# An attention-and-two-layers kernel: another order of the first layer, 65 operations on other engines, 14 dummy products, another order of PSUM tiles, and a wider constant

## The chip, the cores and the metric

The kernel runs on one core of a Trainium2 chip. The metric is the device time of one launch in microseconds (us), the median of the runs; smaller is better. Engines in the profile: PE is TensorE's matmuls and PEld its weight loads, DVE is VectorE, ACT is ScalarE, POOL is GpSimd, SP is SyncE, which here only issues DMA transfers. PEclk is the clock that the throttle granted to TensorE, as a share of full speed.

## The reference

Attention over 32 memory slots, then two layers of a gated kind. Batch 4, 8 heads, 576 positions, head width 64; 2304 tokens, model width 512, inner width 1536.

```python
a = np.exp(phi - np.max(phi, axis=2, keepdims=True))          # over the 576 positions
a = a / (np.sum(a, axis=2, keepdims=True) + 1e-09)
k_m = np.einsum('bhsm,bhsd->bhmd', a, k)
v_m = np.einsum('bhsm,bhsd->bhmd', a, v)
scores = scale * np.matmul(q, k_m.transpose(0, 1, 3, 2))
attn = np.exp(scores - np.max(scores, axis=-1, keepdims=True))
attn = attn / (np.sum(attn, axis=-1, keepdims=True) + 1e-09)
x = np.matmul(attn, v_m)                                       # then to 2304 x 512
x = (x @ w_a) * (x @ w_b) @ w_out                              # first layer
g = x @ w_gate                                                 # second layer
return g * (1.0 / (1.0 + np.exp(-g))) * (x @ w_val) @ w_out
```

The layers' weights arrive as 64-bit floats, seen as pairs of 32-bit words; the kernel turns them into 32-bit floats itself.

## The kernel before, in words

Every operand of a large product is held as two fp32r tiles, a high part and a low one (`hi`, `lo`), and each product is three: high by high, high by low, low by high. One launch has two halves: attention and the first layer, up to about 398 us, and the second layer.

**Weights.** A chunk of weights i.j is loaded by `W` (i is a block of 128 of the inner width, j which of three matrices) and decoded by `chunk`, in steps: absolute value and low word on ACT (L222, L224), a clamp (L228) on DVE or POOL, two DVE operations (L232, L236), an add on POOL (L246 or L248), and for output weights a high part on ACT and a low part (`o_lo`) on POOL.

**Attention**, for each batch b: `att_phi` takes the maximum of phi over the nine groups r of positions (`over_r`, L320 to L326: four operations, of which the first two have 384 elements), transposes it on PE (L336), takes it further on DVE and PE, adds, takes the exponential (L355), and makes k_m and v_m on PE in one bank (L364, called kv in the profile); `att_sum` adds phi's exponentials; then the scaled parts are transposed (L399) and copied out (L406, two copies, on ACT). `att_q` transposes q (L424; 8, 8 and 2 blocks) and copies it; `att_scores` makes the scores of two head pairs on PE (L442 and L452), and takes maximum, exponential, sum and quotient on DVE and ACT. Each batch has two such blocks. `att_out` transposes the weights of attention back (L489).

**First layer.** v_m is multiplied into w_a and w_b first (`vw_part`, L543). `s1_a` and `s1_b` are the products with 288 columns (L528); s1b's result is copied by ACT (L594), multiplied on DVE (L596), and split (L603, and L608 on DVE or POOL). `s2_first` and `s2_part` multiply by w_out (L520, 384 columns) and add into an accumulator, on DVE (L645). `x_ops` makes the operands of the second layer from the accumulators (L671 to L679, high and low parts on DVE and POOL).

**Second layer.** `second` closes the first layer's pools and opens a PSUM pool `ps2` of eight banks. `unit` works through seven products p5, p1, p2, p6, p3, p7, p4 with 288 columns (L776; p_z, p_a and p_c in the profile are their banks), and `s4_tile` is the last product (L520, 512 columns, p_h).

**Order.** The work is written as generators, and `PLAN` is a hand-written list of tokens. Each occurrence of a token runs its generator to the next `yield`: P, K, L, Q and W are loads (phi, k and v of two head pairs, of the other two, q, weights), p the steps of `att_phi`, e `att_sum`, q `att_q`, s `att_scores`, o `att_out`, c a chunk's, v `vw_part`, a and b `s1_a` and `s1_b`, d and f `s2_first` and `s2_part`, x `x_ops`, E `second`, U a `unit`, A and O later loads and H `s4_tile`. At the end `behind` chains the instructions of each engine, SP too, in the plan's order, so each engine's queue is the plan. `STEPS` holds for some operations a letter for the engine of each occurrence (A, V, P). The function `warm` exists, but the plan of before does not use it. A tile of a `ring` takes a buffer of its tag in rotation where `SLOTS` has no entry for it, and `SLOTS` is empty; the tag b2 has four PSUM buffers of two banks each.

`const` holds the identity `ident` (128x128, the moving operand of all transposes) and behind it `ones`, two columns of fp32; all other tiles are placed behind these.

Of the kernel before, what the change touches and what calls it, by code (L numbers as in the profile page):

```python
# [1113 lines left out]
```

## Time and profile before

| what | us |
|---|---|
| median of three runs | 822.45 |
| runs | 824.23, 822.04, 822.45 |
| the profiled execution | 822.6 |
| its span in the trace | 820.8 |
| PE busy | 795.0 (97%) |
| DVE busy | 573.4 (70%) |
| ACT busy | 403.6 (49%) |
| POOL busy | 381.7 (47%) |

The span is the time from the first instruction to the last in the trace of the profiled execution; the rest of its 822.6 lies outside the trace. A busy share is that of instructions that compute or move data on the engine; waits are not in it.

### The profile page before, as it was taken

How to read it: one execution, taken by the hardware profiler on the slowest of the kernel's cores; microseconds unless marked ns; L12 is line 12 of the kernel's file. 1: busy time of each engine (PE TensorE's matmuls, PEld its weight loads, DVE VectorE, ACT ScalarE, POOL GpSimd, SP SyncE). 2: the span in 40 equal slices, each digit the busy share in tenths (PEclk: the TensorE clock that was granted, in tenths of full speed). 3: DMA queues.
4: the chain of work that ended last, by engine and by line, in shares of the span. 5: the costliest groups of instructions: out<-in, count | busy, mean ns of one | idle time of the engine just before them, and what ended most of it. 6: DMA issues, size and time to landing. Idle time of an engine off the chain costs nothing.

```text
span 820.8 us, 16480 instructions
## 1 busy us (share of the span) xinstructions
PE 795.0 (97%) x6540; PEld 745.9 (91%) x6540; DVE 573.4 (70%) x1020; ACT 403.6 (49%) x790; POOL 381.7 (47%) x319
## 2 busy tenths in 40 slices
PE   3799999999999999999899999999999999999997
PEld 2688999999999999999899999999999999999996
DVE  5899967878866777488685767856786455656565
ACT  3556656346434543354467565444464653434331
POOL 1454665545535354355667646544563442424210
PEclk9899999999999999999999999999999999999999
DMA  9984233543433323211456546323233422113004
GB/s 326 378 300 141 91 123 130 174 143 112 143 100 102 105 77 122 72 39 46 128 168 230 163 153 200 108 91 110 91 86 103 129 70 72 47 56 129 20 1 115
DMA packets 61772, 102.51 MB, mean 125 GB/s; under 512 B 6400, under 2 KB 35072, under 8 KB 61696
## 3 DMA queue, kind: packets, MB, share of 16 engines
q1 hardware_dynamic: 60896, 100.29, 37.6%
q8 instruction: 51, 0.84, 0.4%
q10 hardware_dynamic: 800, 1.18, 0.4%
q14 instruction: 25, 0.20, 0.1%
HBM read 82.58 MB, written 18.87 MB: 124 GB/s over the span
## 4 chain that ended last, share of the span: by engine, by line
PE 94%; DMA 2%; DVE 2%; SPq 1%; issue 0%; ACT 0%
PE p_a L776 19%; PE p_h L520 18%; PE s L520 15%; PE p_z L776 9%; PE s1a L528 9%; PE s1b L528 9%; PE p_c L776 5%; PE s L528 3%; PE vw L543 2%; DMA h10x<-in_phi_dram 1%; PE sc L442 1%; DMA h7x<-in_q_dram 1%; PE qT L424 1%; SPq L312 1%; PE kv L364 1%; PE sc L452 0%
## 5 line engine op out<-in xcount | busy, mean ns | idle before, releaser
L520 PE MATMUL p_h<-o,g 128*128 128x512 f32 x648 | 163.2, 393 | 0.0
L520 PEld LDWEIGHTS p_h<-o,g 128*128 128x128 f32 x648 | 117.0, 188 | 21.0 <-DVE h_2x L851 0.2
L520 PE MATMUL s<-gh,o 128*128 128x384 f32 x480 | 125.3, 335 | 0.0
L248 POOL TENSOR_TENSOR dec_a<-dec_a,raw 128x512 int32<-128x512 int32 x48 | 65.3, 1364 | 83.2 <-DVE dec_a L236 47.6
L520 PEld LDWEIGHTS s<-gh,o 128*128 128x128 f32 x480 | 87.0, 188 | 0.8 <-issue 0.4
L851 DVE TENSOR_TENSOR h_2x<-p_h,h_2x 128x512 f32<-128x512 f32 (+1 forms) x100 | 62.1, 633 | 35.8 <-PE p_h L520 35.4
L222 ACT ACTIVATE dec_a<-raw 128x512 f32<-128x512 f32 x72 | 48.4, 677 | 69.4 <-DMA dr_o<-dec_a 16.5
L520 PE MATMUL s<-gl,o 128*128 128x384 f32 x240 | 80.2, 334 | 0.0
L528 PE MATMUL s1b<-h_1x,vwh 128*128 128x288 f32 x384 | 67.6, 298 | 0.0
L528 PE MATMUL s1a<-h_1x,vwh 128*128 128x288 f32 x384 | 67.2, 297 | 0.1
L528 PEld LDWEIGHTS s1b<-h_1x,vwh 128*128 128x128 f32 x384 | 56.5, 188 | 3.5 <-issue 3.3
L246 POOL TENSOR_TENSOR w<-dec_a,raw 128x512 int32<-128x512 int32 x24 | 31.9, 1331 | 59.0 <-DVE dec_a L236 31.9
L528 PEld LDWEIGHTS s1a<-h_1x,vwh 128*128 128x128 f32 x384 | 56.5, 189 | 1.4 <-issue 0.8
L236 DVE SCALAR_TENSOR_TENSOR dec_a<-raw,dec_a 128x512 int32<-128x512 int32 x72 | 53.7, 746 | 2.5
L596 DVE TENSOR_TENSOR bs<-s1a,bs 128x576 f32<-128x576 f32 x48 | 36.0, 753 | 24.6 <-PE s1a L528 22.3
L594 ACT COPY bs<-s1b 128x576 f32<-128x576 f32 x48 | 30.4, 639 | 43.8 <-PE s1b L528 36.5
L161 POOL TENSOR_TENSOR w_g<-again_a,w_g 128x512 fp32r<-128x512 f32 x24 | 31.7, 1322 | 43.4 <-ACT w_g L157 40.8
L161 POOL TENSOR_TENSOR w_u<-again_s,w_u 128x512 fp32r<-128x512 f32 x24 | 31.9, 1328 | 40.8 <-ACT w_u L157 40.8
L827 ACT CAST g<-gate 128x576 fp32r<-128x576 f32 x48 | 32.1, 676 | 36.2 <-PE p_h L520 21.1
L794 DVE TENSOR_TENSOR p_c<-p_c,gate 128x288 f32<-128x288 f32 x48 | 22.1, 465 | 38.6 <-PE p_c L776 27.9
L829 DVE TENSOR_TENSOR g<-gate,g 128x576 fp32r<-128x576 f32 x48 | 38.7, 811 | 14.7 <-ACT g L827 14.2
L603 ACT CAST gh<-bs 128x576 fp32r<-128x576 f32 x48 | 31.0, 673 | 34.0 <-PE s L520 29.9
(224 smaller groups left out, 1943.4 us busy)
## 6 DMA issues: line engine op xcount, KB each, us to landing
raw<-in_moe_w_out_dram SPq DMA_DIRECT2D x24, 512.0 KB, 3.5
again_s<-dr_w SPq DMA_DIRECT2D x24, 512.0 KB, 3.7
dr_w<-dec_a SPq DMA_DIRECT2D x36, 256.0 KB, 3.3
again_a<-dr_w SPq DMA_DIRECT2D x24, 384.0 KB, 3.1
raw<-in_moe_w_b_dram SPq DMA_DIRECT2D x12, 512.0 KB, 4.4
raw<-in_moe_w_a_dram SPq DMA_DIRECT2D x12, 512.0 KB, 3.9
raw<-in_moe_w_val_dram SPq DMA_DIRECT2D x12, 512.0 KB, 3.7
...
```

The source lines that it names most:

```text
L161: nc.gpsimd.tensor_tensor(out=t[:, :, 1], in0=x, in1=f32(t[:, :, 0]), op=ALU.subtract)
L222: nc.scalar.activation(out=f32(a), in_=f32(hi), func=ACTF.Abs)
L236: nc.vector.scalar_tensor_tensor(out=a, in0=hi, scalar=-0x40000000, in1=a, op0=ALU.bitwise_and, op1=ALU.bitwise_or)
L246: nc.gpsimd.tensor_tensor(out=o, in0=ai, in1=li, op=ALU.add)
L248: nc.gpsimd.tensor_tensor(out=a, in0=a, in1=lo, op=ALU.add)
L520: nc.tensor.matmul(dst, lhsT=l, rhs=r, start=(i == 0), stop=(i == n - 1))
L528: nc.tensor.matmul(p[:, hb, 0:HB], l, x, start=(i == 0), stop=(i == n - 1))
L596: nc.vector.tensor_tensor(out=bs, in0=pa_t.pop((b, f)), in1=bs, op=ALU.mult)
L776: nc.tensor.matmul(bank(where), lhsT=x, rhs=y, start=first and t == 0, stop=t == len(terms) - 1, skip_group_check=True,)
L827: nc.scalar.copy(out=hi, in_=v)
L829: tt(out=lo, in0=v, in1=f32(hi), op=ALU.subtract)
L851: tt(out=dst, in0=src, in1=dst, op=add)
```

## The change

1. `SLOTS` is filled: each tile of b2 and of the rings of raw, dec_a, pm, nmx, rs, kvm, w, mx, vwh, den, vwl, bs, o, gh, gl, q, g, s, t, g2 and a22 gets a buffer number of its own, in place of rotation.
2. `ones` is cut from a tile of 32 columns, 128 bytes to a partition in place of 8, so all tiles start at multiples of 128.
3. `o_lo` of the first layer and the copies of k (L406) take their engine from `STEPS`.
4. `STEPS`: 65 operations change engine: 25 from DVE to POOL (9 low parts at L608, 12 clamps, 2 quotient multiplies, 2 sums), 26 from POOL to DVE (7 at L608, 7 `o_lo`, 6 clamps, 4 multiplies, 2 sums), 9 from DVE to ACT (5 q copies, 4 copies of `s2_first`), 5 from ACT to DVE (2 copies of k, 1 q copy, 2 of `s2_first`).
5. `BANKS` gives the order in which the second layer's PSUM tiles are placed.
6. `PLAN` has the same tokens in another order and 14 new ones, z0 to z13, which run `warm`: a product of the identity with itself twice, 256 columns in fp32, into a b2 tile that nobody reads. The order differs up to E, in some 90 tokens behind it and in the middle of the second layer; the last 330 tokens are the same. In the new plan the loads begin P0, P1, L0, W0.1, K0, Q0, W0.0, W1.1, W1.2, K1, L1, Q1, W1.0; before they began P0, L0, W0.1, W0.0, K0, W1.1, Q0, P1, W1.2, K1, L1, W1.0, Q1. The scores s1.1 and s1.0 now come ahead of the first of a and b; before, b0.0 and b0.1 came first.

The tokens that end the first layer's DVE work are, before, f1.3, f1.2, x1, x1, f1.4, E, and now f1.3, f1.4, x1, f1.2, f1.1, E. The first `unit` after E was U0.12 and is U1.12.

```diff
     SLOTS = """
+    b2
...
+    raw
+    0123012301320132010321032130213132313203012023012013203132012302312301301320312031203121203201312032101020210321320230210
+    a 012012102021010102120120101201021022100210100212021021022102021021201102 pm 0101 nmx 0101 rs
+    0101 kvm 0101 w 012301030202130231201302312013023120130231201302312013023120 mx 01010101 vwh
...
-    ones = const.tile([128, 2], FP32, name="ones")
+    ones = const.tile([128, 32], FP32, name="ones")[:, 0:2]
...
-        nc.gpsimd.tensor_tensor(out=l, in0=x, in1=f32(h), op=ALU.subtract)
+        (eng("ol", i) if i < NF else nc.gpsimd).tensor_tensor(out=l, in0=x, in1=f32(h), op=ALU.subtract)
...
-            nc.scalar.copy(out=kb[b % 2][rows, :, :, o], in_=kT[rows])
+            copy(eng("kT", b), kb[b % 2][rows, :, :, o], kT[rows])
...
-    gl VPPVVPPPVVVPPVVVVVPPVVPVPVVVPVPPVVPVPPVVVPVPPPVV rmx VVVV mul PVPVPPPV sub VVVVVVVV sum
-    VPPV qT AAAVAVVAAAVV acc VVVAVAVAAVVVVVVA clamp VVVVVPVPPVVVPPPVVPVVPPVVVVVVVVVVPVVPVVPVVV
+    gl VPVPPVVVVVVVPVPVPVPPPVPPPVVPPVPPVPPVPPVVPVVVPPVV rmx VVVV mul VPVPPVVV sub VVVVVVVV sum
+    PVVP ol PPVVVVVVVPPP kT VAAV qT AAAAVAAAAAAA acc AAAAVAVVAVVVVVAV clamp
+    PVPVPPPPPVVPVPVVVVPVPVPPPVPVPPVVVVVVVVPVVV
...
+    BANKS = "z1 z0 a1 a0 c1 c0 h0 h1"
...
-        for n in ("a0", "c0", "z0", "a1", "c1", "z1", "h0", "h1"):
-            chain.append(ps2.tile([128, 512], FP32, tag=n, name=f"p_{n}"))
+        names = ("a0", "c0", "z0", "a1", "c1", "z1", "h0", "h1")
+        t = {n: ps2.tile([128, 512], FP32, tag=n, name=f"p_{n}") for n in BANKS.split()}
+        chain.extend(t[n] for n in names)
...
-    P0 L0 W0.1 W0.0 c0.1 c0.0 c0.0 p0 p0 K0 p0 c0.1 c0.1 p0 p0 p0 W1.1 c0.0 c0.1 Q0 p0 e0 P1 W1.2
-    p0 c1.1 c0.0 q0.0 p0 c1.1 p0 q0.0 q0.2 K1 p0 p0 q0.1 L1 p1 c1.1 p1 q0.2 p1 p0 p1 c1.1 p0 s0.0
-    W1.0 c0.1 c0.0 q0.1 p1 c1.2 p1 s0.1 s0.0 s0.0 v0 s0.0 s0.1 s0.1 v0 s0.0 s0.0 Q1 p1 v0 c1.1 e1
-    p1 W0.2 s0.0 s0.1 s0.1 P2 c1.0 c1.0 s0.1 s0.1 c1.0 c1.2 o0.1 L2 p1 q1.2 c1.0 p1 o0.1 p1 o0.0
-    o0.0 c0.2 q1.0 o0.1 c1.0 v1 W2.2 p1 q1.2 o0.0 c0.2 v1 p2 p1 b0.0 c1.2 p2 P3 v1 c0.2 b0.1 W4.1
...
+    P0 P1 L0 p1 z6 z7 p0 z9 W0.1 c0.1 p1 z0 K0 p0 p0 Q0 p0 c0.1 p0 z2 z12 z1 p1 p0 W0.0 z10 p1 W1.1
+    p1 W1.2 e0 p0 p0 c0.1 q0.2 c0.1 K1 q0.2 L1 p0 q0.1 p0 p0 c0.0 Q1 p0 z13 q0.1 c0.1 q0.0 c1.1
+    c0.0 q0.0 c1.1 p0 W1.0 s0.1 P2 s0.0 c1.2 z4 p0 W0.2 c0.0 c1.1 z8 c1.1 c0.0 z3 s0.1 z11 c0.0
+    c1.2 K2 p1 s0.1 s0.0 s0.0 s0.1 v0 z5 e1 s0.0 c1.1 v0 c1.2 s0.0 c1.2 p1 s0.1 s0.1 c1.2 p1 p1 v0
+    q1.0 q1.1 p1 q1.0 s0.0 q1.2 c1.0 W2.2 p1 s0.0 p1 s0.1 c1.0 o0.1 o0.0 W4.1 q1.2 o0.1 q1.1 p2 p1
+    c1.0 P3 c0.2 o0.0 c0.2 o0.1 c1.0 c0.2 o0.0 s1.1 s1.1 p2 p2 c1.0 p1 s1.1 s1.0 p2 L2 c1.2 v1 a0.0
...
```

## Rows read from the trace of the kernel before

**Rows 1.** The page, first part: busy us, share of the span, instructions.
```profile
PE 795.0 (97%) x6540; PEld 745.9 (91%) x6540; DVE 573.4 (70%) x1020; ACT 403.6 (49%) x790; POOL 381.7 (47%) x319
```

**Rows 2.** Windows: us; busy of PE, PEld, DVE, ACT, POOL; PEclk; DMA share; GB/s.
```profile
0.00:10.00 10.00, 1.14 (x5) 0.48 (x5) 3.08 (x10) 1.75 (x2) 0.70 (x6) 1.00 0.83 281
10.00:20.00 10.00, 5.84 (x158) 5.37 (x158) 6.86 (x14) 4.99 (x10) 2.57 (x2) 1.00 1.09 369
20.00:30.00 10.00, 7.12 (x96) 5.89 (x95) 6.57 (x13) 5.40 (x9) 2.98 (x3) 0.77 1.05 384
30.00:40.00 10.00, 7.76 (x206) 6.24 (x205) 9.46 (x22) 6.27 (x12) 5.10 (x6) 0.89 1.06 374
40.00:50.00 10.00, 10.00 (x113) 9.07 (x113) 9.19 (x18) 6.51 (x12) 4.57 (x5) 1.00 0.93 317
...
400.00:450.00 50.00, 50.00 (x350) 48.41 (x350) 33.84 (x70) 37.15 (x84) 36.75 (x33) 1.00 0.52 166
```

**Rows 3.** Waits of PE: what it waited for; us in total, times, longest.
```profile
PE mx L336 <- DVE pm L326: 9.1, 2, 6.8
...
PE p_z L776 <- DVE h8x L645: 2.6, 1, 2.6
```

**Rows 4.** The chain that ended last: start us, us, what ran.
```profile
25.97 1.05 PE sc L442 x16
...
39.90 1.59 PE s1b L528 x12
...
47.14 0.87 PE qT L424 x8
48.02 0.61 PE sc L442 x16
48.63 0.23 PE sc L452 x4
...
395.46 2.01 DVE h_x0x L679 x3
397.46 0.88 DVE h8x L645
```

**Rows 5.** Timeline of SP's queue: start us, us, issue of the second q.
```profile
18.87 7.13 SPq L312 DMA_DIRECT2D h5x<-in_q_dram  x2
```

**Rows 6.** DMA view: the same q's larger part, its size, us to landing.
```profile
h5x<-in_q_dram SPq DMA_DIRECT2D x1, 1024.0 KB, 14.7
```

**Rows 7.** Timeline of ACT in the front.
```profile
37.73 0.73 ACT L222 ACTIVATE dec_a<-raw 128x512 f32<-128x512 f32 x1
...
40.02 0.74 ACT L406 COPY kb<-kvT 64x256 f32<-64x256 f32 x2
```

**Rows 8.** Lines, the clamp on either engine: busy us, mean ns; idle before.
```profile
L228 DVE TENSOR_SCALAR dec_a<-dec_a 128x512 f32<-128x512 f32 x61 | 33.9, 563 | 4.5 <-ACT dec_a L222 4.5
L228 POOL TENSOR_SCALAR dec_a<-dec_a 128x512 f32<-128x512 f32 x11 | 21.6, 1965 | 11.4 <-ACT dec_a L222 11.4
```

**Rows 9.** Timeline of DVE ahead of the second layer.
```profile
397.38 0.95 DVE L645 TENSOR_TENSOR h8x<-s,h8x 128x768 f32<-128x768 f32 x1
```

**Rows 10.** Timeline of POOL and DVE at 13 us; in brackets idle before, releaser.
```profile
13.45 1.28 POOL L246 TENSOR_TENSOR w<-dec_a,raw 128x512 int32<-128x512 int32 x1 [12.15 <-DVE dec_a L236]
13.90 1.25 DVE L323 TENSOR_TENSOR rm<-h9x 128x384 f32<-128x384 f32 x1 [0.59 <-ACT h9x L355]
15.18 0.56 DVE L324 TENSOR_TENSOR rm<-rm,h9x 128x384 f32<-128x384 f32 x1
```

**Rows 11.** The chain again: long products of the second layer.
```profile
674.40 3.22 PE p_a L776 x24
...
805.67 10.90 PE p_h L520 x48
```

**Rows 12.** Timeline of PE: two blocks of vw products, eight at a time.
```profile
51.35 1.09 PE L543 MATMUL vw<-w,vt 64*32 64x256 f32 x32
...
105.48 0.64 PE L543 MATMUL vw<-w,vt 64*32 64x256 f32 x16
```

More of the change, by code (lines that the diff above doesn't have):

```diff
@@ new lines @@
+    b0.8 c10.2 f0.3.6 c10.2 c11.1 v15 v15 f0.1.6 c9.2 f0.2.6 W10.1 c11.0 c10.0 f0.4.6 c9.2 v15
+    c10.0 c10.0 b0.8 f0.5.6 b1.8 f0.1.6 c10.2 c10.1 W17.1 W11.2 c11.0 b1.9 b0.9 c10.2 b0.9 f0.2.6
+    A0.12 a3.8 c10.2 c10.1 f0.5.6 c11.0 c10.0 f0.4.6 a0.9 b2.8 b0.8 b1.9 c10.2 b0.9 v15 b3.8 b1.8
+    v15 W17.0 f0.4.8 b0.9 c11.0 f0.4.8 c11.0 b2.9 a2.8 b3.8 c11.2 c11.2 c11.2 c10.1 b0.9 f0.5.8
+    f0.2.8 f0.3.8 c11.2 b2.8 c10.1 c10.1 f0.5.8 v16 b2.8 c11.2 b3.8 c17.1 c17.1 f0.1.8 f0.0.8 b2.9
+    b3.9 f0.3.8 A0.12 W18.1 f0.2.8 c17.1 f0.1.8 A0.12 a2.9 c17.0 a3.9 A0.12 v16 f0.0.8 v16 b2.8
@@ new lines @@
+    A0.14 U1.13 U0.13 U0.13 U0.13 A0.15 U1.13 U0.14 A0.14 c19.2 U1.13 U0.14 O0.14 U0.13 c19.1 U0.14
+    U0.14 A0.14 U1.13 A0.15 U1.14 U1.13 c19.2 c19.1 U1.14 U1.14 U0.13 c19.1 U0.14 A0.15 A0.15
+    H0.13.0 U0.14 c19.1 U1.13 c19.1 c19.2 U0.14 c19.2 U0.14 U1.14 U1.13 U0.14 U0.14 U1.14 c19.2
+    U1.14 H0.13.1 U0.14 U1.14 U0.14 U0.14 U1.14 U1.14 H0.13.0 c19.0 W20.1 U1.14 U0.14 U1.14 O0.14
+    U0.14 U1.14 O0.15 A0.15 A0.15 U1.14 U1.14 H0.13.1 U1.14 H0.13.2 A0.15 c19.2 U1.14 c19.1 U1.14
+    U1.14 U0.14 U1.14 U0.15 A0.15 U1.14 U0.14 c20.1 U1.15 U0.14 H0.13.2 U0.15 U0.14 A0.15 U0.14
@@ new lines @@
+    A0.20 U0.19 U1.19 U1.19 U0.19 O0.19 A0.20 H0.17.6 H0.17.5 U1.19 H0.17.6 U1.19 U0.19 U0.19
+    H0.17.8 O0.20 U1.20 U0.19 c23.0 U0.20 c23.1 A0.20 H0.17.5 A0.20 U0.19 U0.20 c23.0 H0.17.7 U0.19
+    U1.20 U1.19 A0.20 U0.20 U1.19 U0.19 U1.19 A0.20 U1.19 U0.20 U0.20 H0.17.8 U1.20 U1.19 A0.20
+    A0.21 U1.20 U0.19 U0.20 A0.21 A0.22 U1.20 U1.20 U0.20 A0.21 U0.20 U1.20 A0.21 H0.19.0 A0.21
+    U0.20 H0.19.0 U1.20 U1.20 A0.21 U1.20 U0.20 A0.21 U0.20 U0.20 U1.20 U0.20 c23.0 U1.20 H0.19.2
+    U1.20 U1.20 U1.20 U1.20 U0.20 U0.20 U1.20 c23.2 U0.20 U1.21 U0.20 c23.1 A0.21 H0.19.2 U1.21
@@ new lines @@
+    U3.12 U3.12 U2.12 U3.12 U3.12 x3 U2.12 x3 U3.12 H0.23.6 U2.12 U2.13 U2.13 U3.12 U2.13 U2.13
+    H0.23.5 U3.12 U3.12 U3.12 O1.12 A1.13 H0.23.6 U2.13 U3.13 U2.12 U3.12 U3.13 A1.16 H0.23.7 U3.12
+    U3.13 U2.13 A1.13 U3.12 U2.13 U3.13 A1.13 U2.13 U2.13 A1.13 U3.12 U2.13 A1.14 A1.14 H0.23.7
+    U3.13 U2.13 U3.13 U3.13 U3.13 U3.13 U2.13 U2.13 U3.13 U3.13 U2.13 H0.23.8 U3.13 U2.13 U3.13
+    U3.13 U2.13 A1.14 U3.13 O1.13 U3.13 A1.14 H0.23.8 U2.13 U3.13 U2.13 A1.14 U2.14 U2.13 O1.17
+    U2.14 U2.13 U3.13 U3.14 U3.14 U3.13 U2.13 U2.14 U3.14 U2.14 U2.14 U3.13 U3.14 U3.13 H1.13.0
@@ new lines @@
+    H1.13.4 A1.16 H1.13.5 U3.15 A1.16 A1.16 A1.16 U3.15 A1.16 O1.15 U3.15 U2.15 H1.13.6 A1.16
+    H1.13.6 U3.15 A1.17 U2.16 U3.15 U3.15 U3.16 U2.16 U3.15 U3.16 U3.15 H1.13.8 U2.15 U2.15 U3.16
+    U2.15 H1.13.7 U3.15 U3.16 U3.15 U2.16 U3.16 U3.16 U2.16 U3.16 O1.16 U2.16 U3.16 U2.16 x3
+    H1.13.8 U2.16 U2.16 x2 U3.16 U2.16 H1.13.7 U3.16 A1.17 U2.16 U3.16 U3.16 U2.16 U2.16 U2.16
+    H1.15.0 O1.21 O1.17 A1.17 U2.16 U3.16 U3.16 U2.16 H1.15.1 O1.18 H1.15.0 A1.17 U3.16 U3.16 U3.16
+    U2.16 U2.16 U2.16 H1.15.1 U2.16 A1.19 U3.16 U3.17 A1.17 U2.16 U3.17 O1.17 U2.17 A1.18 U2.17
@@ new lines @@
+    O1.20 A1.22 U3.21 U3.21 U3.20 U2.21 U2.21 U3.21 U2.21 U3.21 U2.21 U3.21 H1.19.3 H1.19.4 A1.22
+    U2.21 H1.19.5 U3.21 U2.21 U3.21 U2.21 A1.23 U3.21 U2.21 H1.19.5 U3.21 A1.22 U2.21 H1.19.6 U3.21
+    A1.23 U3.21 U2.21 H1.19.6 U2.21 O1.23 U2.21 H1.19.8 O1.23 U3.21 U2.21 H1.19.8 U2.22 U2.22 U3.21
+    H1.19.7 U3.22 U2.22 U3.21 U2.21 U2.22 U3.22 O1.22 U3.21 H1.19.7 U3.21 U2.22 U2.21 A1.22 U3.21
+    U2.22 U3.22 U3.22 U3.22 U3.21 U3.22 A1.22 U2.22 U2.22 H1.21.1 U2.22 A1.23 U3.22 H1.21.0 H1.21.0
@@ new lines @@
+    U2.22 U3.22 A1.23 U2.22 U2.22 U2.22 U3.22 U3.22 U2.22 U3.22 H1.21.1 H1.21.2 U2.22 U2.22 U3.22
+    U2.22 U2.22 H1.21.3 A1.23 H1.21.3 U2.23 A1.23 U3.22 U2.23 U3.22 U2.22 U3.22 U2.23 U3.22 A1.23
+    U3.22 U2.22 U2.23 A1.23 U2.23 H1.21.2 A1.23 U2.22 U2.23 U3.22 U3.23 U2.23 U2.23 U2.23 U3.23
+    U3.22 U3.22 U2.23 U2.23 U3.23 H1.21.4 U2.23 H1.21.4 H1.21.5 U3.22 U2.23 U3.23 U2.23 U3.23
+    H1.21.5 U3.23 U2.23 U2.23 H1.21.6 U2.23 O1.22 U3.23 H1.21.7 H1.21.6 H1.21.8 U2.23 U3.23 U2.23
+    U2.23 H1.21.8 U3.23 U3.23 U3.23 U2.23 U3.23 U3.23 U3.23 H1.21.7 U3.23 H1.23.0 U3.23 U3.23
```

302 lines of the change are left out of this document (134 added, 168 removed).

## The prediction

> **What bounds the kernel now.** The page's first part comes first: TensorE (PE) is busy 97% of the span, VectorE (DVE) 70% [rows 1]. So only PE's gaps and the length of its products can give time. Three views say where the gaps are. In the windows [rows 2] PE is busy 1.14 and 5.84 us of the first two tens, 7.12 and 7.76 of the next two, then all of 40 to 50, and all of a later stretch too. The waits [rows 3] name two places: 9.1 us for phi's maxima on DVE in the front, and 2.6 at the seam of the two layers. The chain [rows 4] shows the order: scores of batch 0 at 25.97, the first product of the first layer (s1b) at 39.90, the transposes of the next q and the scores of batch 1 only behind it, at 47.14 and 48.02. In the first 40 us the DMA engines are full (share 0.83 to 1.09), and by 30 DVE is busy 9.2 to 9.5 of every 10 [rows 2]: loads set the start, DVE the stretch behind it, and later PE alone.
>
> **The front: plan order and loads.** The plan loads phi 1 second, and so takes the maxima, exponentials and sums of batch 1 early; the scores of batch 1, in two blocks, now stand ahead of the first s1 product. What gates them is a load, q 1. It is issued at 18.87 [rows 5] and its larger part lands 14.7 us later [rows 6], at 33.6. The second pair's k and v have the same bytes ahead of them on SP's queue in both plans, only in another order, so I leave them where they are. Ahead of q 1 there is one chunk of 0.5 MB less (W1.0 moved behind it), at 374 GB/s [rows 2] 1.4 us: 32.2. From there I follow the new queues. Eight q transposes twice, 0.87 each [rows 4]: 34.0. The last q transposes and the transposes of k's products, by the same 109 ns each, 0.7: 34.7. ScalarE (ACT) then has in plan order a chunk's absolute value (0.73), its low word the same, a q copy of half a pass and a cast (together about 0.9, an estimate by that 0.73), and k's two copies 0.74 [rows 7], in all 3.1, of which 0.6 can run before: 37.2. Two blocks of scores for each of two halves are 4 x (0.61 + 0.23) = 3.4 [rows 4]: 40.6. A v product in front, 0.5 (0.64 for sixteen, end to end [rows 12]): first s1 product at 41.1. That is 1.2 later than the 39.90 of before, with 3.4 of scores and 0.87 of transposes done that stood behind it. So PE has won 3.4 + 0.87 - 1.2 = 3.1, of which I count 2.9, since small products run longer if they come early: scores took 1.05 per sixteen at 25.97, in a stretch granted 0.77, against 0.61 [rows 2, 4]. Bounds: nothing, if the loads slip as DMA stays full, and 5.4, if q 1 and ACT are not late at all.
>
> **40 to 100 us.** Here DVE decides. By 40 us it will have done about 3.4 us more than before, batch 1's maxima and sums, six operations of 0.56 [rows 10], for which it had idle time: 3.14 in 10 to 20 and 3.43 in 20 to 30 [rows 2]. Of the 65 operations with another engine, those of this stretch are, off DVE, five clamps (5 x 0.56 = 2.8 [rows 8]), and on to it one multiply, two k copies and, net, a q copy (+1.5, an estimate by two times the 0.74 of a pair of copies [rows 7]). Net 1.3 us less on DVE. A clamp on POOL (GpSimd) takes 1.97 [rows 8], five of them 9.8, and POOL has only 4.6 to 5.1 of 10 busy [rows 2]. So DVE is up to 4.7 us ahead; PE can turn this into time only where it waits for DVE, and its gaps are small by then, 2.24 in 30 to 40 and none in 40 to 50 [rows 2]. I take 1.7, bounds 0 and 3.4.
>
> **The seam.** PE waits 2.6 us ahead of the second layer [rows 3]: DVE is still in three lo's (2.01) and one accumulation (0.88) when PE has done its last first-layer product [rows 4]. In the new order more stands behind that product: the accumulation f1.4, two lo's, then f1.2 and f1.1, then E. From PE's end DVE has 0.88 + 2 x 0.67 + 2 x 0.95 = 4.1 us [rows 4, 9]. The first layer's PSUM pool comes free as a whole, and z1, z0 now take the banks in which f1.1's tile stands: a wait of 4.1 in place of 2.6, +1.5. If only an earlier tile of the same bank gated, the wait would be nothing: -2.6. I take +1.5, since in the trace the wait ended with the very last accumulation.
>
> **Dummies.** Fourteen products of 256 columns, two instructions each. By the transposes, eight in 0.87 or 109 ns per 128 columns [rows 4], an instruction takes 0.22 and the fourteen 6.1 us, at half clock 12.2. They stand among the phi maxima and the loads, where PE idles 13.0 us in the first 20 and 2.9 in the next ten [rows 2]. Cost 0 while the loads gate; 6.1 if that cover is gone. What they can give is clock: 20 to 30 is granted 0.77 on average [rows 2], a part at 1.2 GHz and a part at 2.4; scores of batch 0 at 0.61 would save 0.44 per sixteen [rows 4], and q 1 comes no sooner for it, so I count nothing.
>
> **Slots, banks, the rest of the second layer.** Explicit slots let a PSUM tile follow its predecessor after two tiles where it was always four; an accumulation of 0.88 to 0.95 [rows 4, 9] fits under one s1 product of PE (1.59 for twelve matmuls [rows 4]), so 0; if DVE were late, each such place would cost some 0.5. BANKS and the order of units touch a stretch in which PE is busy 50.00 of 50.00 [rows 2] and change none of its products: 0, with that work as cover; if a unit's operand came late there, DVE's 0.67 or 0.95 would show. Sums, multiplies and copies of later batches lie under PE: 0; what they cost without that cover is the second rival.
>
> **Sum.** Against the profiled execution's own 822.6 (span 820.8 and 1.8 outside; median of the runs 822.45): -2.9 - 1.7 + 1.5 = -3.1, so 819.5. Its own range is 816.5 to 821.8: the front and the stretch halfway to either bound (1.25 + 0.85 down, 1.45 + 0.85 up) and, downward, a seam shorter by 0.9; the far end is 822.6 - 5.4 - 3.4 - 2.6 = 811.2. About 0.3%, 2.5 us, is what a measurement can tell from no change: 820.0 to 824.9 counts as none.
>
> **Rivals.** *Given back.* DVE is the limit behind the front, and being ahead at 40 means nothing if POOL, with 9.8 us of clamps more, hands over weights later. Then only the seam is left: 822.6 + 1.5 = 824.1. For it: DVE's 9.19 to 9.46 of ten [rows 2]; against it: its early idle time is used.
>
> *Slower, by collisions of DVE and POOL.* While POOL's add of 13.45 ran, DVE's maximum took 1.25; the next one of the same size, after it, 0.56 [rows 10]. Twenty-five operations go from DVE to POOL and run 1.3 to 2 us each there [rows 8, 10], so more of DVE's work meets one. A meeting costs up to 0.69. It decides from about ten more of them in the DVE-bound stretch: DVE has 0.5 to 0.8 of ten spare there [rows 2], so of 7 us PE loses nearly all, and with the seam's 1.5 and the front's 2.9 back, 827 to 828. Against it: only five of the moved clamps lie in that stretch. The Trainium skill, SBUF — State Buffer, section "SBUF: two separate sides", tells of ports that DVE and GpSimd share and lock against each other; the 1.25 and 0.56 agree with it, and it speaks against moving work to POOL.
>
> *A denser front and no seam:* 822.6 - 2.9 - 1.7 - 2.6 = 815.4, with the front's 5.4 it is 813; 813 to 816.
>
> *Alignment.* The wider `ones` moves all that is placed behind it. PE's long products take N/2.4 ns and a rest: 24 of 288 columns in 3.22 us are 134 ns, 120 and 14; 48 of 512 in 10.90 are 227, 213 and 14 [rows 11]. The transposes, whose moving operand is the identity, placed ahead of `ones`, take 109, which is 256 steps and 2 ns [rows 4]. If the rest came from where the moving tile starts, and 11 to 14 of 134 to 227 went away, 5 to 10% of the 716 us behind 100 would go: 36 to 72, so about 770. Against it: the vw products read moving tiles behind `ones` too, and a set of eight at 256 columns takes 0.22 (two more sets, 1.09 against 0.64 [rows 12]), next to 512 steps or 0.213; a shifted start by itself costs them nothing that shows. They are of another type (fp32, not fp32r), so the rival isn't excluded. The Trainium skill, TensorE: Matmul & The Clock Gate, section "Back-to-back issue gap", gives N/2.4 + 2.5 ns for bf16 at full clock; the transposes' rest agrees, the 14 ns of these products does not, and no row here says why.
>
> **Chances.** Forecast 0.45; given back 0.18; collisions 0.13; denser front 0.12; alignment 0.12. The predicted time is the forecast's. To hold 8 in 10 the range takes in all but alignment and the thin ends, the far end and 828 with a us or two more: 809 to 829. Faster by over 0.3% are about two thirds of the forecast's case (0.29, as 816.5 to 820.0 is 3.5 of its 5.3 us), the denser front and alignment: 0.53. Slower: the collisions and a sixth of the given-back case, 0.16. The rest, 0.31, is no change.
>
> **What would show it.** The first L528 product at about 41 us with all of batch 1's scores ahead of it, and a granted clock nearer 1.00 in 20 to 30; if it starts after 44, the front's step is wrong. DVE's busy share in 40 to 50 about as before. Ahead of the first p_z a wait of about 4 us for an L645; under 2.6, the seam's step is wrong. 288 columns still 134 ns; if about 122, the alignment rival holds, and the sum above is the small part. Many DVE rows above 1.2 us for 384 elements would show collisions. The prediction is wrong if the time is under 816 or over 824.

## The result, and the profile after

The changed kernel takes 829.52 us (median of six runs, 828.2 to 834.47) against 822.15 for the kernel before: ratio 1.0108, 95% interval 1.0090 to 1.0125. The forecast was 819.5, in a range of 809 to 829: wrong in sign, and just outside the range. The profiled execution is of 829.43, span 827.6. Two executions far from all others (1118 us at a granted clock of 0.65 under all_fixes, 1313 us at 0.56 under all_kT) are left out of the medians and ratios below.

The page's first part of the changed kernel [rows 1]:

```profile
PE 805.0 (97%) x6568; PEld 750.1 (91%) x6568; DVE 572.2 (69%) x1019; ACT 405.8 (49%) x792; POOL 384.0 (46%) x318
```

PE is busy 10 us longer; the dummies, 28 instructions that take 10.9 us by the timeline, account for it. The windows of the changed kernel [rows 2], and behind them those that lost PE time later on:

```profile
10.00:20.00 10.00, 8.83 (x175) 6.58 (x175) 5.66 (x12) 3.50 (x7) 3.96 (x5) 0.76 1.07 400
20.00:30.00 10.00, 9.67 (x195) 7.22 (x199) 8.98 (x18) 8.17 (x13) 6.65 (x5) 1.00 1.05 397
30.00:40.00 10.00, 7.60 (x159) 5.94 (x141) 9.68 (x22) 6.09 (x13) 5.58 (x4) 1.00 1.06 400
40.00:50.00 10.00, 9.55 (x120) 7.79 (x120) 9.79 (x18) 6.13 (x12) 4.53 (x4) 1.00 1.07 393
...
150.00:200.00 50.00, 47.45 (x411) 44.93 (x410) 36.94 (x50) 21.61 (x34) 26.05 (x22) 1.00 0.44 138
...
350.00:400.00 50.00, 47.67 (x303) 47.35 (x301) 42.80 (x56) 21.43 (x35) 23.63 (x17) 1.00 0.21 68
400.00:450.00 50.00, 47.49 (x322) 46.47 (x323) 32.98 (x68) 32.72 (x74) 30.57 (x27) 0.93 0.50 156
```

DVE is at 9.7 to 9.8 of 10 from 30 to 50, the loads run at 397 to 400 GB/s from 10 to 40 us in place of 369 to 384, and there are three places of lost PE time that the forecast did not have or had too small: 2.55 us in 150 to 200, the seam, and a clock under 1.00 behind it. PE's waits [rows 3] name them:

```profile
PE mx L349 <- DVE pm L339: 4.9, 2, 4.3
PE p_z L792 <- DVE h7x L659: 4.8, 1, 4.8
PE s1a L542 <- DVE h8x L659: 2.3, 1, 2.3
```

To add them up I compare how much of PE's work is done at the same moment: each product counted at its usual start-to-start time (0.132 us for 288 columns, 0.173 for 384, 0.231 for 512, 0.109 for a transpose, small ones at their mean), dummies at nothing. Us of work ahead of the kernel before (minus: behind), by the profiled executions:

```
moment us         40   100   165   180   390   420   800
after            1.6   0.9   1.1  -2.3  -1.9  -6.1  -6.8
ones32           3.7   3.7   3.7   3.6   3.8   2.3   2.3
seam             1.1  -4.5  -4.2  -5.4  -5.6  -4.9  -5.6
evac_first       1.7  -0.1   0.1  -2.1  -1.7  -6.1  -6.8
raw_early        1.2  -0.4  -0.3  -1.8  -1.2  -6.1  -7.2
all_no_dummies   1.2   0.1   0.3  -1.8  -1.2  -0.5  -1.6
ones32_seam      3.7   4.0   4.1   4.0   4.0   5.1   5.2
before_seam      1.5   1.5   1.5   1.5   1.5   2.6   2.7
seam_warm        1.4  -0.3  -0.2  -2.2  -1.7  -5.1  -5.9
no_dummies       1.7   0.3   0.3  -2.1  -1.4  -6.0  -6.7
```

The row of before_seam tells how far such a row can be trusted: up to the seam its program is that of the kernel before, and it is 1.5 ahead all the same. A difference of 1.5 us between two single executions in the front shows nothing.

In this execution of the changed kernel the front wins 1.1, which is within that spread, the place at 170 loses 3.4, 0.4 come back by 390, the seam and what follows it lose 4.2 (-1.9 at 390 to -6.1 at 420), and the rest 0.7, of which a wait of 0.48 for an L867, ended at 600, is the larger part. In eight of the twelve traces of the new order PE also stands 0.9 to 2.5 us somewhere between 67 and 75 with nothing in the trace that it waits for; why stays open.

**The front.** PE from its timeline (in brackets the idle time before and what ended it): all its waits over 0.2 us between 31 and 43 us, and the first product of the first layer.

```profile
34.24 0.44 PE L437 MATMUL qT<-ident,h5x 128*128 128x128 f32 x2 [0.94 <-DVE vwl L582]
35.44 0.52 PE L412 MATMUL kvT<-ident,kvm 128*128 128x128 f32 x3 [0.77 <-DVE kvm L403]
37.15 0.77 PE L502 MATMUL aT<-ident,h9x 128*128 128x128 f32 x5 [0.41 <-DVE h6x L529]
43.07 0.79 PE L542 MATMUL s1a<-h_1x,vwh 128*128 128x288 f32 x4
```

The transposes of q 1 begin at 31.35, so its load is there by then. What PE waits for after that is DVE, 2.1 us in three places.

**The seam.** DVE and PE there, from the timeline of the changed kernel (in brackets the idle time before and what ended it), then the clock in its windows:

```profile
397.71 0.96 DVE L659 TENSOR_TENSOR h8x<-s,h8x 128x768 f32<-128x768 f32 x1 [1.06 <-PE s L534]
398.58 1.31 DVE L693 TENSOR_TENSOR h_x0x<-h_1x,h_x0x 128x576 fp32r<-128x576 f32 x1
399.82 0.75 DVE L693 TENSOR_TENSOR h_x0x<-h5x,h_x0x 128x576 fp32r<-128x576 f32 x1
400.49 0.54 DVE L659 TENSOR_TENSOR h7x<-s,h7x 128x384 f32<-128x384 f32 x1
400.96 0.54 DVE L659 TENSOR_TENSOR h8x<-s,h8x 128x384 f32<-128x384 f32 x1
401.42 0.94 DVE L659 TENSOR_TENSOR h7x<-s,h7x 128x768 f32<-128x768 f32 x1
...
402.51 3.22 PE L792 MATMUL p_z<-h_x0x,w_u 128*128 128x288 f32 x12 [4.84 <-DVE h7x L659]
```

```profile
397.50:400.00 2.50, 0.17 (x1) 0.00 (x0) 2.29 (x3) 0.00 (x0) 1.70 (x3) 1.00 0.00 0
400.00:402.50 2.50, 0.00 (x0) 0.02 (x1) 2.36 (x4) 0.00 (x0) 0.00 (x0) 0.59 0.89 269
402.50:405.00 2.50, 2.49 (x10) 2.50 (x11) 0.00 (x0) 0.00 (x0) 0.00 (x0) 0.50 0.43 151
405.00:407.50 2.50, 2.50 (x14) 2.50 (x13) 0.00 (x0) 1.52 (x5) 0.40 (x1) 0.55 0.01 3
```

The queue is the one forecast: f1.4, two lo's, f1.2 (two pieces), f1.1. But PE stood 4.84 us, and then its first products ran at a granted clock of 0.50 to 0.55, the 1.2 GHz level: twelve took 3.22. In the profile before, a wait of 2.57 was followed by 1.00.

**The place at 170.** From the timeline of the changed kernel, SP's queue, DVE and PE, with one piece of the chain:

```profile
160.74 3.26 SPq L222 DMA_DIRECT2D raw<-in_moe_w_out_dram  x2
164.04 0.43 SPq L288 DMA_DIRECT2D dr_w<-dec_a  x1
...
170.13 0.43 DVE L241 TENSOR_SCALAR dec_a<-dec_a 128x512 f32<-128x512 f32 x1 [4.08 <-ACT dec_a L235]
...
172.67 0.79 PE L542 MATMUL s1a<-h_1x,vwh 128*128 128x288 f32 x4 [2.28 <-DVE h8x L659]
```

```profile
164.04 5.32 DMA dr_w<-dec_a
```

A store stands behind a load on SP; it lands after 5.32 us; ACT's next chunk waits for the tile that the store reads; DVE waits 4.08 us for ACT with other work queued behind the clamp; PE waits for the accumulation in that queue.

**Products and loads.** In the chain of the changed kernel, the same kinds of products as in [rows 4, 11]:

```profile
681.28 1.59 PE p_a L792 x12
...
812.55 10.90 PE p_h L534 x48
```

12 of 288 columns in 1.59 are 133 ns, 48 of 512 in 10.90 are 227: the wider `ones` changed no product.

### The profile page after: what moved, and what is told of

It reads as the page before. It is cut to its first block, busy times and chain, and to the rows that moved or that the text cites. A ratio compares the mean times of both kernels' runs of the same rounds, so it can differ in the third digit from the quotient of the medians.

```text
span 827.6 us, 16519 instructions
## 1 busy us (share of the span) xinstructions
PE 805.0 (97%) x6568; PEld 750.1 (91%) x6568; DVE 572.2 (69%) x1019; ACT 405.8 (49%) x792; POOL 384.0 (46%) x318
## 4 chain that ended last, share of the span: by engine, by line
PE 88%; DVE 6%; DMA 2%; issue 2%; POOL 1%; ACT 1%; SPq 0%; POOLq 0%; ACTq 0%
PE p_a L792 19%; PE p_h L534 18%; PE s L534 13%; PE p_z L792 9%; PE s1b L542 8%; PE s1a L542 8%; PE p_c L792 5%; PE s L542 3%; PE vw L557 2%; DMA dr_w<-dec_a 1%; DVE dec_a L249 1%; DMA h10x<-in_phi_dram 1%; DVE dec_a L245 1%; PE sc L455 1%; PE kv L377 1%
## 5 line engine op out<-in xcount | busy, mean ns | idle before, releaser
L867 DVE TENSOR_TENSOR h_2x<-p_h,h_2x 128x512 f32<-128x512 f32 (+1 forms) x100 | 62.0, 632 | 33.6 <-PE p_h L534 33.4
L622 POOL TENSOR_TENSOR gl<-bs,gh 128x576 fp32r<-128x576 f32 x23 | 34.3, 1497 | 35.3 <-ACT gh L617 35.2
L237 ACT ACTIVATE raw<-raw 128x512 int32<-128x512 uint32 x72 | 48.3, 678 | 0.0
L608 ACT COPY bs<-s1b 128x576 f32<-128x576 f32 x48 | 30.3, 641 | 36.0 <-PE s1b L542 28.6
```

Source lines behind the costliest of these rows:

```text
L237: nc.scalar.activation(out=lo, in_=lo.bitcast(U32), func=ACTF.Copy, scale=2.0 ** -29)
L622: eng("gl", B * f + b).tensor_tensor(out=g[1], in0=bs, in1=f32(g[0]), op=ALU.subtract)
L867: tt(out=dst, in0=src, in1=dst, op=add)
```

## The experiments

Ratios are against the kernel before, measured beside each on the same chip. Those of the changed kernel, 829.52 and 1.0108, are the ones above. Where an edit is in `PLAN`, the tokens are shown that move, cut out of its lines.

**seam**: the last accumulations ahead of the lo's.

```diff
-    f1.3.10 f1.4.10 x1 f1.2.10 f1.1.10 E
+    f1.3.10 f1.2.10 f1.1.10 f1.4.10 E x1
```

> The changed kernel with its last first-layer tokens in another order: the accumulations f1.2 and f1.1 ahead of f1.4's, the two lo's of x1 behind E. Theory: PE's 4.84 us ahead of the second layer are DVE's queue behind f1.4 (two lo's 2.06, f1.2 1.08, f1.1 0.94), and the half clock of the 4 us behind it is the price of the long idle stretch. DVE then has f1.2, f1.1 and f1.4 left: wait about 2.0, 2.8 less, and no half clock, 2.1 less: 824.6 in place of 829.5. Rival 1, the clock falls at the seam whatever the wait: 826.7. Rival 2, something else gates the second layer (its operands or weights): 829.5.

Measured: 827.22, ratio 1.0056 (1.0034 to 1.0077), that is 4.3 us less than the changed kernel by the ratios. Waits and one window of this run:

```profile
PE p_z L792 <- DVE h8x L659: 1.8, 1, 1.8
```

```profile
402.50:405.00 2.50, 1.81 (x14) 1.84 (x15) 2.00 (x3) 0.00 (x0) 0.72 (x1) 1.00 0.33 116
```

The wait is 1.78, the clock stays at 1.00, and in the table the loss of 4.2 becomes a gain of 0.7. The theory of the seam holds, and both rivals fall; the time of 824.6 was missed by 2.6. The last two accumulations and PE behind them tell what the wait is for:

```profile
401.24 0.95 DVE L659 TENSOR_TENSOR h7x<-s,h7x 128x768 f32<-128x768 f32 x1
402.10 0.94 DVE L659 TENSOR_TENSOR h8x<-s,h8x 128x768 f32<-128x768 f32 x1
403.19 1.83 PE L792 MATMUL p_z<-h_x0x,w_u 128*128 128x288 f32 x12 [1.78 <-DVE h8x L659]
```

Here f1.1 (h7x) is done at 402.19 and PE starts only behind f1.4 (h8x). In the changed kernel f1.4 was done at 398.67 and PE started only behind f1.1. Both tiles are in use at once and so in different buffers: PE waits for the whole pool, not for one bank, in whatever order `BANKS` places the banks.

In this execution another thing shows, between 36 and 50:

```profile
37.50:40.00 2.50, 2.50 (x30) 1.99 (x30) 2.40 (x6) 2.45 (x6) 1.52 (x2) 0.50 1.08 389
40.00:42.50 2.50, 2.50 (x37) 2.00 (x33) 2.35 (x5) 1.15 (x2) 1.78 (x2) 0.50 1.05 401
```

The clock is at half for some 14 us, and 4 to 5 us of the front are gone (1.1 at 40, -4.5 at 100). The program up to there is that of the changed kernel, whose profile has 1.00 in the same windows: from one execution to the next the clock falls here or not. That is where the missing 2.6 us went, as far as this one trace tells; two of the six runs, at 823.83 and 824.24, are at the time expected.

**seam_warm**: eight dummies more in the seam's gap, all in one PSUM buffer.

```diff
-    f1.3.10 f1.4.10 x1 f1.2.10 f1.1.10 E
+    f1.3.10 f1.4.10 x1 f1.2.10 f1.1.10 z20 z21 z22 z23 z24 z25 z26 z27 E
```

> The changed kernel with eight more dummy products on PE between its last first-layer product and the second layer (3.5 us in the 4.84 us gap); DVE's queue is as it was. Theory that the half clock behind the seam comes of PE's idle stretch: clock 1.00 behind the seam, the wait for DVE unchanged in its end, 2.1 less: 827.4. Rival, the half clock comes with the new products or with anything but idleness: 829.5. If the dummies themselves last past DVE's end: above 829.5.

Measured: 828.61, ratio 1.0088 (1.0063 to 1.0113), 1.6 less by the ratios, not clear of the changed kernel's interval. The trace says why it is not more:

```profile
397.35 5.90 PE L731 MATMUL warm<-ident 128*128 128x256 f32 x16
403.35 1.84 PE L792 MATMUL p_z<-h_x0x,w_u 128*128 128x288 f32 x12
```

Sixteen dummy instructions take 0.37 us each and last 1.2 past DVE's end, but the products behind them take 1.84 in place of 3.22: with PE kept busy the clock did not fall. So of the seam's loss of 4.2 us 2.3 were the longer wait (4.84 against 2.57) and the rest, some 2, the clock.

**store_first**: the store ahead of the load on SP.

```diff
-    W13.2 c13.2 c13.1
+    c13.1 W13.2 c13.2
```

> The changed kernel with one token moved by two places: the last step of chunk 13.1, which issues the store of chunk 13.0's tile, ahead of the load W13.2. Theory: the 2.28 us in which PE stands at 170 come from SP's queue, where that store (its data done at 162.37) stands behind a load that waits for its raw buffer until 163.66; the store lands at 169.36, the next chunk's absolute value waits for the tile, DVE for it, PE for DVE. Store 1.6 earlier, gap 0.7: 827.9, or down to 826.6 if it lands sooner and what follows the gap (0.4 at 179) goes too. Rival, the store's landing is set by the DMA queue and not by its issue: 829.5.

Measured: 828.79, ratio 1.0100 (1.0071 to 1.0128): no clear difference. The store was issued in time, but now the load, issued at 168.43, landed 4.19 us later and held ACT; DVE still waited 3.12 us for ACT and PE 1.34 for DVE. The rival was nearer, though it is a load's landing and not the store's.

**vp_undone**: 23 of the 25 operations that went from DVE to POOL are back on DVE.

```diff
-    gl VPVPPVVVVVVVPVPVPVPPPVPPPVVPPVPPVPPVPPVVPVVVPPVV rmx VVVV mul VPVPPVVV sub VVVVVVVV sum
-    PVVP ol PPVVVVVVVPPP kT VAAV qT AAAAVAAAAAAA acc AAAAVAVVAVVVVVAV clamp
-    PVPVPPPPPVVPVPVVVVPVPVPPPVPVPPVVVVVVVVPVVV
+    gl VPVPVVVVVVVVPVVVVVPPPVPVPVVVPVPPVVPVPPVVVVVVPPVV rmx VVVV mul VVVVPVVV sub VVVVVVVV sum
+    VVVV ol PPVVVVVVVPPP kT VAAV qT AAAAVAAAAAAA acc AAAAVAVVAVVVVVAV clamp
+    VVVVVPVPPVVVVPVVVVVVPVVVVVVVVVVVVVVVVVPVVV
```

> The changed kernel with 23 of its 25 operations that went from DVE to POOL back on DVE (all twelve clamps, seven of the nine low parts, the multiplies and the sums). Theory that the lost time sits in the seam and in one store: these operations cost nothing that counts, and DVE has less spare time without POOL: 829 to 832. Rival, collisions of DVE with POOL's longer operations took back what the front won: 823 to 827, with DVE's mean times shorter.

Measured: 840.74, ratio 1.0236 (1.0215 to 1.0258), 11 us slower than the changed kernel. Windows of 40 to 100 us, the changed kernel first, then this one:

```profile
40.00:100.00 60.00, 59.04 (x963) 50.96 (x962) 55.02 (x102) 41.28 (x74) 35.72 (x26) 1.00 0.51 177
```

```profile
40.00:100.00 60.00, 54.42 (x894) 46.22 (x890) 55.70 (x106) 38.25 (x69) 21.39 (x15) 1.00 0.45 153
```

PE loses 4.6 us there while DVE is as busy as before: DVE sets this stretch, and what counts is how much work it has. Whatever collisions with POOL cost, it is less than what these operations save; as the reason for the loss the collision rival is out. Its 827 to 828 us came nearest to the measured time, by chance.

**evac_first**: the accumulation ahead of the clamp on DVE.

```diff
-    c14.0 b1.4 b0.4 a0.4 c8.2 c14.0 a1.4 f1.5.2
+    f1.5.2 c14.0 b1.4 b0.4 a0.4 c8.2 c14.0 a1.4
```

> The changed kernel with one token of DVE moved: the accumulation f1.5.2 ahead of chunk 14.0's clamp. In the run with the store moved the stall at 170 stayed, as the chunk before, 13.2, then waited for its own load, issued at 168.43 and landed 4.2 later. Theory now: what stops PE there is DVE's queue, in which the accumulation that frees PE's bank stands behind a clamp that waits for ACT, and ACT for a load or a store, whichever. With the accumulation ahead PE has no wait there: 2.28 less by the profile of the changed kernel, 0.45 to 1.34 by those of the three later runs; 828.0, between 827.2 and 829. Rival, PE needs the chunk's own work a little later: the wait moves behind 173, and the time stays 829.5.

Measured: 828.60, ratio 1.0074 (1.0060 to 1.0089). The median fell by 0.9, the ratio by 0.0034, and the intervals just part. But in the trace the rival is right: a wait of 1.26 for an L610, ended at 179.83, takes the place of the one at 170, and at 180 this run is 2.1 behind, as the changed kernel is (2.3).

**no_dummies**: the 14 z's left out, with their PSUM buffers' numbers.

```diff
-    P0 P1 L0 p1 z6 z7 p0 z9 W0.1 c0.1 p1 z0 K0 p0 p0 Q0 p0 c0.1 p0 z2 z12 z1 p1 p0 W0.0 z10 p1 W1.1
+    P0 P1 L0 p1 p0 W0.1 c0.1 p1 K0 p0 p0 Q0 p0 c0.1 p0 p1 p0 W0.0 p1 W1.1
...
```

> The changed kernel without its 14 dummy products (and without their PSUM buffers). If their cover holds, nothing is lost by them, and they may hold the clock: 829.5 or above, with a granted clock under 1.00 in 20 to 32 as in the kernel before. If the eight dummies between 25.4 and 28.9 stand in front of batch 1's kv product, which has its data: up to 3 less, 826.5. If DVE sets the stretch to 100 us in any case, no change: 829.5 within 1.

Measured: 828.89, ratio 1.0078 (1.0064 to 1.0091): no loss without them, rather a gain, of 0.6 by the medians and 2.5 by the ratios, whose intervals just touch. Windows of this run:

```profile
25.00:27.50 2.50, 0.77 (x20) 0.18 (x16) 2.43 (x4) 1.81 (x3) 2.50 (x3) 1.00 1.05 402
27.50:30.00 2.50, 1.97 (x76) 2.00 (x84) 2.40 (x6) 1.16 (x2) 1.84 (x1) 0.61 1.11 371
30.00:32.50 2.50, 2.50 (x90) 2.30 (x75) 2.43 (x5) 0.00 (x0) 0.94 (x1) 0.70 1.08 408
```

The clock falls at about 28, where it stays at 1.00 in the changed kernel's profile. PE is about where it is in the changed kernel later (0.3 ahead at 100, 2.1 behind at 180), and DVE is at 2.4 of 2.5 throughout.

**ones32**: the kernel before with the wide `ones` alone.

```diff
-    ones = const.tile([128, 2], FP32, name="ones")
+    ones = const.tile([128, 32], FP32, name="ones")[:, 0:2]
```

> The kernel before with nothing but the wider ones, so that all tiles start at multiples of 128 bytes. Alignment rival: 288 columns in 122 ns, about 770. The reading of the changed kernel's trace, in which 24 of 288 columns take as long as before: 822.2, no change. A third case: loads land sooner (the changed kernel moved 400 GB/s in 10 to 40 us, the kernel before 369 to 384); then up to 2 less, 820.

Measured: 820.24, ratio 0.9972 (0.9957 to 0.9988). The third case. Its windows:

```profile
10.00:20.00 10.00, 6.19 (x155) 5.84 (x156) 7.32 (x15) 4.83 (x9) 2.57 (x2) 1.00 1.07 399
20.00:30.00 10.00, 7.66 (x207) 6.26 (x212) 9.57 (x19) 7.36 (x13) 4.83 (x6) 1.00 1.06 399
30.00:40.00 10.00, 8.94 (x141) 7.49 (x123) 9.65 (x23) 6.66 (x15) 4.32 (x4) 1.00 1.06 398
```

Against 369, 384 and 374 [rows 2] the loads move 4 to 8% more, and PE is 3.7 us ahead by 40. Part of the 3.7 can be spread between executions, and the kernel before had a granted clock of 0.54 from 25 to 30 in its profile. Runs in which the clock was 1.000 over the whole are free of that: three with the wide `ones` took 818.23 to 818.27, three of the kernel before beside them 820.25 to 820.65, a gain of 2.2. In this execution 1.5 of them are lost again behind the seam, where the clock fell with the same wait of 2.57:

```profile
395.00:397.50 2.50, 2.50 (x13) 2.50 (x12) 0.00 (x0) 1.38 (x3) 0.38 (x1) 0.53 0.04 10
```

**before_seam**: the kernel before with its last lo's behind E.

```diff
-    f1.3.10 f1.2.10 x1 x1 f1.4.10 E
+    f1.3.10 f1.2.10 f1.4.10 E x1 x1
```

> The kernel before with the seam's order changed as in the run called seam: the last lo's of x1 behind E, so that DVE has only accumulations left when PE ends the first layer. Theory: the wait of 2.57 falls to about 1.2, 0.88 for the last accumulation and the semaphore around it: 820.8 in place of 822.2. Rival, the seam there is set by something else: 822.2. If the lo's come too late for the second layer's fourth product: a wait of up to 1 inside it, 821.8.

Measured: 819.74, ratio 0.9969 (0.9956 to 0.9981), 2.5 less. The wait is 1.05, and the theory holds. In the trace the edit is worth 1.1 (1.5 at 390 to 2.6 at 420), and so it is in the runs with a clock of 1.000, 819.36 and 819.39 against 820.25 to 820.65. The rest of the 2.5 goes with the clock, which is below 1.000 in most runs of the kernel before; where it fell in those runs isn't on record.

**raw_early**: POOL's add of chunk 8.2 ahead of chunk 13.1's sums.

```diff
-    c13.1 W14.2 v10 b2.2 f0.4.2 b3.2 b2.2 b2.3 f0.0.2 f0.3.2 W13.2 c13.2 c13.1 c8.2
+    c8.2 c13.1 W14.2 v10 b2.2 f0.4.2 b3.2 b2.2 b2.3 f0.0.2 f0.3.2 W13.2 c13.2 c13.1
```

> The changed kernel with one token of POOL moved: the last step of chunk 8.2 (POOL's add, which frees its raw buffer) ahead of chunk 13.1's sums, which wait for a store to land. With the accumulation first, the wait had only moved to 178, and four variants stood level with each other at 180, 2.0 to 2.3 behind the kernel before; so theory: a ring of waits sets that place, store to POOL (idle 3.26 until 158.79), POOL to raw buffer (163.63), buffer to load (issue 163.66, landed near 168.7), load to ACT, DVE and PE. POOL's add then runs near 156.7, the load is issued near 161.1 and the stall of 2.3 goes: 827.3. Rival, the second W load waits for something else or DVE is late there in any case: level with the others at 180, 829.5.

Measured: 829.99, ratio 1.0112 (1.0088 to 1.0136): no gain. In the trace the loss between 165 and 180 is 1.5 in place of 3.4, as DVE waits 2.18 for ACT and not 4.08, but this execution came to 165 behind (-0.3) and had won only 0.5 by 180. Nor is the 1.5 clearly the edit's: the runs seam, seam_warm and no_dummies, which change nothing at this place, lose 1.3, 2.0 and 2.4 there (seam from -4.2 to -5.4 with a wait of 0.45 for PE and 2.33 for DVE). What is lost at 170 differs from one execution to the next, and a gain by this edit isn't shown.

**after_ones2**: the changed kernel with `ones` as before.

```diff
-    ones = const.tile([128, 32], FP32, name="ones")[:, 0:2]
+    ones = const.tile([128, 2], FP32, name="ones")
```

> The changed kernel with ones as it was, two columns, so that all tiles stand 32 bytes past multiples of 128 again; everything else as changed. In the kernel before the wide ones gave 2.3 us and 399 in place of 369 GB/s in 10 to 20 us. If the loads set the front of the changed kernel too: 831.8. If DVE sets it, as its 9.7 of 10 from 30 to 50 say: 829.5, with 370 to 385 GB/s all the same. If the ring at 170 levels out whatever the front does: 829.5, but a smaller lead at 100.

Measured: 834.77, ratio 1.0136 (1.0111 to 1.0161). Three of five runs were at 834.8 to 835.0 with a granted clock of 0.987 or 0.988 over the whole, the other two at 829.8 and 830.4. In 10 to 40 us it moved 375 GB/s, the changed kernel 399, the kernel before 376, ones32 399: this goes with the wide `ones` and not with the order. The two others lie 0.3 and 0.9 above the changed kernel's median; the three are 5 above it, as the runs with a half clock in 36 to 50 are (this kernel's profile, one of them, is 5.2 behind at 100). One in six runs of the changed kernel is of that kind too, so five runs do not tell what the wide `ones` are worth there; the three outcomes expected are not told apart.

**ones32_seam**: both small edits on the kernel before.

> The kernel before with the wide ones and with the seam's order changed (the last lo's of x1 behind E), and nothing else. One gave a ratio of 0.9972, the other 0.9969; they sit at opposite ends of the first layer, so they should add: 817.3, faster than either kernel. If the front's gain is lost behind the seam, 819.7.

Measured: 817.30, ratio 0.9950 (0.9935 to 0.9965). They add. At a clock of 1.000 the two such runs, 816.66 and 817.23, are some 3.5 below the 820.45 to 820.57 of the kernel before beside them, close to the sum of 2.2 and 1.1. This is the fastest of all, 12 us faster than the changed kernel and 4 to 5 faster than the one before.

**seam_raw**: seam and raw_early on the changed kernel.

> The changed kernel with the seam's order and the early raw buffer together. By the trace the seam is worth 4.7 to 5.0 and the ring 2.2: 829.5 - 4.8 - 2.2 = 822.5, level with the kernel before; then the new order, engines, dummies and the wide ones together bring nothing against 822.2. Rival, the front of the new plan loses some more in executions whose clock falls in 36 to 50: 824 to 826.

Measured: 824.59, ratio 1.0052 (1.0031 to 1.0072). Eight of twelve runs lie at 822.8 to 825.5, the other four at 827.8 to 830.6 with clocks of 0.989 to 0.992; the median is the rival's. Against the run seam alone (1.0056) raw_early adds nothing that shows.

**all_fixes**: seam, raw_early, store_first and evac_first together.

> The changed kernel with four reorderings: the seam's, the early raw buffer, the store ahead of the load, and the accumulation ahead of the clamp. If the place at 170 is a ring of two transfers, all its links are now shorter or off PE's way: no PE wait over 0.5 between 165 and 182, and the trace ends level with or up to 1 ahead of the kernel before; 821 to 822 where the clock stays at 1.00 in 36 to 50, 828 to 830 where it falls, as in 4 of 12 runs of the two-fold version, so a median of 822 to 824. Rival, something else holds that place: 165 to 182 still lose 1.5, and 823.5 at best.

Measured: 823.81, ratio 1.0026 (1.0010 to 1.0043), within the 822 to 824 expected. No trace shows the places in it, and its interval overlaps that of seam alone (1.0034 to 1.0077).

**all_no_dummies**: the same without the z's.

> The same without the 14 dummies. The changed kernel without its dummies had no run above 829.3 in six, while versions with them had one to three of six some 5 us above the rest, with a half clock from 36 to 50. If the dummies only shift where the clock falls (to 27 to 32 without them, where a load and DVE are waited for anyhow): 822 with a spread under 2. If they have nothing to do with it: the same spread of 6 as with them.

Measured: 824.49, ratio 1.0040 (1.0026 to 1.0054), seven runs within 824.2 to 826.8. The spread is 2.6; with dummies it is 5 to 8 in most versions, but 1.8 in evac_first. The time is no better. That the dummies shift where the clock falls isn't shown: in this profile it falls between 37 and 40.5, as in raw_early with dummies, and not between 27 and 32. The profile shows what is left at 170 with all four reorderings: the loss from 165 to 180 is still 2.1, with a wait of 1.02, ended at 179.38, for an L610 behind two chunks' decoding on DVE.

**all_kT**: all_fixes with all copies of k on ACT.

```diff
-    kT VAAV
+    kT AAAA
```

> The four reorderings, with dummies, and the copies of k of batches 0 and 3 back on ACT (0.74 us off DVE before 40 us). If DVE sets the new front, PE's lead at 60 grows by up to 0.7 against the run with the four alone, and so does the time's; if loads or ACT set it, the lead is the same or smaller by what ACT has more.

Measured: 827.15, ratio 1.0062 (1.0047 to 1.0077), 3.3 slower than all_fixes. In its timeline PE waits 2.51 us, up to 24.96, for the copies of batch 0's k on ACT, a wait that the changed kernel has not. So ACT's queue, and not DVE's time alone, sets the new front before 30 us, and batch 0's copies belong on DVE; batch 3's were not tried apart.

## Why the prediction was wrong

**The front and 40 to 100 us** (-2.9 and -1.7): 1.1 measured, not 4.6, and 1.1 is within the spread of the front. Of the forecast's steps the earlier q 1, the scores ahead of s1 and PE's fuller first 30 us are all in the trace (2.5 ahead at 25). The first step that failed is the path to the first s1 product: forecast at 41.1 by way of ACT's queue, it came at 43.07, and the 2.1 us of waits on the way are all for DVE. The second is that from DVE's lead to PE's: "DVE is up to 4.7 us ahead" was counted as time that PE could use, but DVE was the limit from 25 us on, at 9.6 to 9.8 of 10 from 30 to 60 (8.9 from 60 to 100), and 0.9 was left at 100. For the front that is the rival "given back". Faster loads, which the forecast hadn't, are part of even this: with the narrow `ones` (after_ones2) PE's lead at 30 is 1.1, with the wide ones 1.8 to 2.1 in seven traces of the new order. How much the order alone is worth in the front can't be told closer: where the clock fell in 36 to 50, the lead was negative.

**The seam** (+1.5): the mechanism was right and the size was not. By the trace it is 4.2: the wait 4.84 (0.7 more than the 4.1, nearly all of it a lo that took 1.31 and not 0.67; POOL was busy then, but the trace doesn't show that it is why), so 2.3 more than before, and about 2 at half clock behind it, which the forecast left out altogether. The run seam, which changes four tokens, gives 4.3 back. `BANKS` was the reason named for it; by the run seam the pool as a whole gates, and the place of f1.1's tile has no part in it. `BANKS` was not tried alone.

**Slots** (0): this step failed outright. "If DVE were late, each such place would cost some 0.5" had the right condition and a wrong price: at 170 DVE was late by 4.08 us, and 3.4 were lost in this execution, 1.3 to 2.4 in others with the same program there. In the trace the order of stores, loads and raw buffers precedes it; and evac_first, which took the wait for the PSUM tile away, was as far behind at 180 (2.1), with a wait for an operand 7 us later. But `SLOTS`, which places the raw buffers too, was not tried alone, so its share isn't shown. Four reorderings did not remove the place: 2.1 are lost there in all_no_dummies, with DVE's decoding crowded into 170 to 179. What would remove it stays open.

**Dummies** (0): right, price and all. Eight instructions in a row, in the changed kernel at half clock and in all_kT at a clock of 1.00:

```profile
11.96 3.34 PE L731 MATMUL warm<-ident 128*128 128x256 f32 x8
28.36 1.99 PE L731 MATMUL warm<-ident 128*128 128x256 f32 x8
```

Those that follow each other directly start 0.43 and 0.22 us apart, the forecast's two prices, and all 28 take 10.9 us, between its 6.1 and 12.2. (The 0.37 of seam_warm is of dummies that all go into one buffer.) Without them the time is the same or 0.6 to 2.5 better. That they hold the clock isn't shown: without dummies it fell at 28 in no_dummies, and not before 37 in all_no_dummies.

**Alignment**: the rival as put is wrong (133 ns per 288 columns stays), but the wide `ones` is worth 2.2 to 2.3 us by another way, the loads. It is the one part of the change that is shown to help in the kernel before.

**Collisions**: out as the reason for the loss, by vp_undone. In the new order 23 of the 25 operations on POOL save about 11 us.

The sum from the profile of the changed kernel is then +1.1 in the front, -3.4 at 170, +0.4 up to the seam, -4.2 there, -0.7 behind it: 6.8 us behind at the end, which is the difference of the spans (827.6 and 820.8). all_fixes leaves 2.2 us against the kernel before, and 6.5 against ones32_seam, which has the wide `ones` and a short seam without the rest: that is what order, engines, slots and dummies cost there together. How it divides among them is not shown.
